# One visit a tile for the local attention jobs, and softmaxes four steps apart, in a fused attention and feed-forward kernel

## The chip, the cores and the metric

The kernel runs on one core of a Trainium2 chip. The core has a matrix engine (TensorE, called PE in the profile, with its weight loads as PEld), a vector engine (VectorE, DVE), a scalar engine (ScalarE, ACT), GpSimd (POOL) and SyncE (SP), whose queue issues the DMAs. The metric is the time of one execution on the device in microseconds (us); lower is better.

## The reference

Eight batches of eight heads, 576 positions, 64 channels, all float32. The first four heads of each batch attend to the last 32 positions (local); the other four attend to the earlier positions that are equal to the query's modulo 32 (strided). The attention output, 4608 tokens of 512 channels, goes through a feed-forward layer with an exact GELU of width 2048.

```python
def _attn_ref(q, k, v):
    stride = 32
    scores = (1.0 / np.sqrt(D)) * np.matmul(q, k.transpose(0, 1, 3, 2))
    rel = pos[:, None] - pos[None, :]
    mask_local = (rel >= 0) & (rel < stride)
    mask_strided = (rel >= 0) & (pos[None, :] % stride == pos[:, None] % stride)
    masks = [mask_local if h < H // 2 else mask_strided for h in range(H)]
    scores = np.where(masks, scores, -1e9)
    attn = softmax(scores)               # with 1e-9 added to the sum
    return np.matmul(attn, v)

def _moe_ref(x, w_in, w_out):            # x: 4608 x 512, from the attention
    h = x @ w_in
    g = 0.5 * h * (1.0 + erf(h / sqrt(2)))
    return g @ w_out
```

## The kernel before, in words

**Tiles and steps.** The 4608 tokens are 12 tiles of 384 (`TT`). The feed-forward layer has 16 blocks (`NF`) of 128 hidden units, so there are 192 steps; step `n` is block `n % 16` of tile `n // 16`, and `ready[t] = 16 t` is the first step of tile `t`. Numbers are split into a high and a low part, so each product takes three matmuls: `ffn_h(n)` (L602 to L604) makes 12 matmuls into one of two PSUM banks `H`; `ffn_g(n)` lets ACT apply the GELU in place (L611) and copy the high part `gh` (L613), and DVE subtract to the low part `gl` (L615); `ffn_o` (L641 to L643) makes 9 matmuls of step `n - 2` into the output banks `O0` to `O2`. Because `H` has two banks, `ffn_h(n + 2)` may begin only when `gl` of step `n` has been read out of its bank. At the end of a tile ACT copies the output out (L648) and SP stores it.

**Strided attention** is done on DVE, in units: dot products (L477), a softmax whose exponential is on ACT (L487), weighted sums (L517, L519), a transpose (L527) and the split into the tile's high and low part `xh`, `xl` (L231 on ACT, L233 on DVE). `run_strided` hands out this work step by step. Exponentials that are pending are issued by `flush_exps`; a GELU after an exponential needs another activation table (the ACT_TABLE_LOAD rows).

**Local attention** is done in jobs of 128 tokens, three to a tile (`JPT`), for tiles 2 to 11 by `band_job` (tiles 0 and 1 are done in the opening part by an order written out by hand). A job has seven parts, each ended by a `yield`: 0, the scores, 32 matmuls of 32 columns by 64 (L290) into the score banks `S0` and `S1`, of which job `i` uses columns `128 i` to `128 i + 127`; 1, the row extremes on DVE (L304); 2, the exponentials on ACT (L308); 3, sum, reciprocal, product and transpose on DVE (L311 to L314), and eight small DMAs (L319) that lay the probabilities out as a band; 4, the values, 16 matmuls (L328) into a bank `X`; 5, the copy of `xh` on ACT (L231); 6, the difference `xl` on DVE (L233). Of a tile, jobs 0 and 1 write their values to bank `X`, and job 2 takes a fresh tile in the bank of `S0`.

**What sets the order.** In the steady part, from step 16 on, the order of PE and of ACT is the order in which the program issues; the order of DVE, SP and POOL is left to a planner. `step(n)` first calls `visit(n)`, then `run_strided`, then `ffn_h(n)`, `ffn_g(n)` and `ffn_o(n - 2)`. `visit` does the local work of a step: for tile `t`, the scores and row extremes of all three jobs at step `ready[t-1] + 2`; the exponentials of job `i` `2 i + 1` steps later and part 3 `2 i + 2` steps later; the values and the split at `ready[t-1] + 12`. So PE leaves the feed-forward matmuls twice a tile, once for 96 matmuls and once for 48.

```python
SCORES, VALUES = 2, 12
score_at = {ready[t - 1] + SCORES: t for t in range(2, NTILE)}
value_at = {ready[t - 1] + VALUES: t for t in range(2, NTILE)}
```

Of the kernel before, what the change touches and what calls it, by code (L numbers as in the profile page):

```python
# [10 lines left out]
F32 = mybir.dt.float32  # L11
# [12 lines left out]
P = 128  # L24
STRIDE = 32
TT = 384
LU = 64
# [56 lines left out]
def attn_ffn_kernel(ctx: ExitStack, tc: tile.TileContext, qk, vl, qka, va, qs, ks, vs, w, out):  # L84
    nc = tc.nc
    NJ = qk.shape[0]
    NR, D = qs.shape[2:]
    S = NR * STRIDE
    HL = P // STRIDE
    NT, DM = out.shape  # L90
    NF = w.shape[0]
    NC = DM // P
    NU = len(PLACE)
    NV = len(VISITS)
    NTILE = NT // TT
    NS = NTILE * NF
    JPT = NJ // NTILE
    SC = 1.0 / (D ** 0.5)
    DH = D // 32
    N2 = HL // 2  # L100
# [20 lines left out]
    def rows(j):  # L121
        return slice(j * D, (j + 1) * D)
# [107 lines left out]
    def to_x(dh_, dl_, src):  # L230
        nc.scalar.copy(dh_, src)  # L231
        yield
        nc.vector.tensor_tensor(dl_, src, dh_.bitcast(F32), ALU.subtract)  # L233

    def local_job(x, banks=None, dve=0, pn=-1):
# [35 lines left out]
        dst = [a[:, 0:N2, c0:c0 + P] for a in x_tile(t)]  # L271
        yield from to_x(*dst, xv)

    def band_job(x, bt, sx):

        QB = STRIDE
        i = x % JPT
        if i == 0:  # L280
            sx["s"] = [ps_a.tile([P, DM], F32, name=f"S{j}_L{x}", tag=f"S{j}") for j in range(2)]
        s = [t[:, i * P:(i + 1) * P] for t in sx["s"]]
        qv = jq[x][:, 0:2 * N2 * LU].rearrange("p (r a t) -> p r a t", r=N2, a=2)
        kv = jq.pop(x)[:, 2 * N2 * LU:].rearrange("p (r a t) -> p r a t", r=N2, a=2)
        head = [(h % 2, slice(h // 2 * 2 * QB, (h // 2 + 1) * 2 * QB)) for h in range(HL)]
# [16 lines left out]
        for h in range(HL):  # L302
            j, cs = head[h]
# [14 lines left out]
                kb = g % 2 + c  # L318
                nc.sync.dma_start(bt[kb * QB:(kb + 1) * QB, g, :], tv[g * QB:(g + 1) * QB, c, :])  # L319
        yield  # L320
        if i % 2 == 0:
            sx["x"] = ps_a.tile([P, DM], F32, name=f"X_L{x}", tag="X" if i == 0 else "S0")
        xv = sx["x"][:, i % 2 * N2 * P:(i % 2 + 1) * N2 * P].rearrange("p (r q) -> p r q", r=N2)
        bv = bt.rearrange("p (a b) (h q) -> p a b h q", a=2, h=HL)
        for r in range(N2):
            for a in range(2):
                for j in range(2):
                    nc.tensor.matmul(xv[rows(j), r, a * LU:(a + 1) * LU], jv[x][:, a, 2 * r + j, :],  # L328
                                     bv[:LK, a, :, 2 * r + j, :], start=True, stop=True)
        jv.pop(x)  # L330
        load_jv(x + 3)
        yield
        t, c0 = divmod(x * P, TT)
        dst = [d[:, 0:N2, c0:c0 + P] for d in x_tile(t)]
        yield from to_x(*dst, xv)


    ka = {}
# [120 lines left out]
    def flush_exps(u):  # L459
        while exps and exps[0][0] <= u:  # L460
            exps.pop(0)[1]()
# [298 lines left out]

    SCORES, VALUES = 2, 12
    score_at = {ready[t - 1] + SCORES: t for t in range(2, NTILE)}
    value_at = {ready[t - 1] + VALUES: t for t in range(2, NTILE)}
    banks = {}
    local = {}
    band = slot("band", [P, 4 * DM])
# [4 lines left out]
    def part(x, *which):  # L773

        for p in which:
            if p == 0:
                local[x] = [band_job(x, bts[x % NBT], banks), 0]
            assert local[x][1] == p
            local[x][1] += 1
            if next(local[x][0], True) is not None:  # L780
# [111 lines left out]
```

## Time and profile before

| | us |
|---|---|
| runs | 888.6, 890.39, 4788.15 |
| median of the runs | 890.39 |
| the profiled execution: time | 890.2 |
| the profiled execution: span, first to last instruction | 888.4 |
| PE busy in the span | 860.2 (97%) |
| DVE busy | 714.1 (80%) |
| ACT busy | 461.2 (52%) |

The time of the profiled execution is 1.8 us more than its span; the trace shows nothing of that rest. The opening part with the hand-written order takes about the first 114 us; the 192 steps end at about 884 us. A "visit" below is one place at which PE does local matmuls between two steps.

### The profile page before, as it was taken

The page shows a single profiled execution, that of the slowest core. Times are in us where ns is not written, and L with a number is a line of the kernel's source. Part 1 is how long each engine was busy: PE and PEld are TensorE (multiplying, and loading weights), DVE is VectorE, ACT ScalarE, POOL GpSimd, SP SyncE. Part 2 cuts the span into 40 slices and gives each one's busy share as a digit, 9 for nine tenths or more (in the row PEclk, how much of TensorE's full clock was granted, in tenths as well). Part 3 has the DMA queues.
Part 4 walks back from the last instruction along what each step waited for, and adds up shares of the span by engine and source line. Part 5 has one row for each costly group of instructions (what it writes and reads, how often), then busy time and mean ns, then how long its engine had stood idle before and what let it go on. Part 6 is the DMA issues. An engine that isn't in the chain of part 4 may idle for free.

```text
span 888.4 us, 19181 instructions
## 1 busy us (share of the span) xinstructions
PE 860.2 (97%) x5948; PEld 771.0 (87%) x5948; DVE 714.1 (80%) x4894; ACT 461.2 (52%) x983; POOL 16.3 (2%) x86
## 2 busy tenths in 40 slices
PE   5499999999999999999999999999999999999998
PEld 4488889889889889988898988988888988999997
DVE  5999999689969989949989969969979988675111
ACT  5999765256446257246346436536534632733222
POOL 4000000000000000000000000000000000000000
PEclk9699999999999999999999999999999999999999
DMA  9992120221030213103022122012113011100101
GB/s 321 363 362 83 48 87 19 81 81 44 29 134 14 61 40 104 36 2 114 12 75 88 40 75 84 16 55 81 61 34 105 16 61 36 31 18 0 37 1 36
DMA packets 33399, 66.27 MB, mean 75 GB/s; under 512 B 6416, under 2 KB 15376, under 8 KB 31248
## 3 DMA queue, kind: packets, MB, share of 16 engines
q1 hardware_dynamic: 33296, 65.04, 22.6%
q8 instruction: 47, 0.77, 0.4%
q14 instruction: 56, 0.46, 0.2%
HBM read 51.64 MB, written 9.44 MB: 69 GB/s over the span
## 4 chain that ended last, share of the span: by engine, by line
PE 91%; DVE 4%; DMA 3%; ACT 1%; SPq 0%; issue 0%; DVEq 0%
PE H L602 15%; PE O L642 15%; PE H L604 15%; PE O L643 15%; PE H L603 15%; PE O L641 14%; DMA ws<-in_w_dram 2%; PE X_L L328 2%; DMA vl<-in_vl_dram 1%; PE S_L L290 1%; DVE acc L519 1%; DVE junk L477 1%; DVE ws L154 0%; DVE w L164 0%; DVE ws L156 0%
## 5 line engine op out<-in xcount | busy, mean ns | idle before, releaser
L611 ACT ACTIVATE H<-H 128x384 f32<-128x384 f32 x192 | 91.4, 476 | 352.8 <-PE H L604 315.6
L602 PE MATMUL H<-xh,w 128*128 128x384 f32 x768 | 262.5, 342 | 4.5 <-DVE gl L615 3.2
L604 PE MATMUL H<-xh,w 128*128 128x384 f32 x768 | 260.0, 338 | 0.0
L603 PE MATMUL H<-xl,w 128*128 128x384 f32 x768 | 259.2, 337 | 0.7 <-DVE xl L233 0.7
L519 DVE SCALAR_TENSOR_TENSOR acc<-sv,sc,acc 128x64 f32<-128x64 f32 x1158 | 258.3, 287 | 0.6
L643 PE MATMUL O<-w,gl 128*128 128x512 f32 x576 | 228.2, 396 | 0.0
L642 PE MATMUL O<-w,gh 128*128 128x512 f32 x576 | 227.7, 395 | 0.0
L641 PE MATMUL O<-w,gh 128*128 128x512 f32 x576 | 224.8, 390 | 0.0
L477 DVE CUSTOM_DVE_ANT_0 junk<-sq,sk 128x64 f32<-128x64 f32 x1290 | 214.5, 228 | 6.3 <-DMA sk<-in_ks_dram 6.2
L615 DVE TENSOR_TENSOR gl<-H,gh 128x384 fp32r<-128x384 f32 x192 | 107.4, 560 | 113.1 <-ACT gh L613 112.1
L602 PEld LDWEIGHTS H<-xh,w 128*128 128x128 f32 x768 | 144.9, 189 | 14.7 <-DVE gl L615 4.1
L603 PEld LDWEIGHTS H<-xl,w 128*128 128x128 f32 x768 | 145.0, 189 | 8.3 <-DVE xl L233 1.1
L604 PEld LDWEIGHTS H<-xh,w 128*128 128x128 f32 x768 | 144.9, 189 | 0.0
L643 PEld LDWEIGHTS O<-w,gl 128*128 128x128 f32 x576 | 108.1, 188 | 23.1
L642 PEld LDWEIGHTS O<-w,gh 128*128 128x128 f32 x576 | 108.3, 188 | 18.3
L641 PEld LDWEIGHTS O<-w,gh 128*128 128x128 f32 x576 | 108.5, 188 | 17.5
L477 DVE DVE_READ_ACCUMULATOR2_ANT sc<- 128x1 f32 x1290 | 118.8, 92 | 0.0
L613 ACT CAST gh<-H 128x384 fp32r<-128x384 f32 x192 | 92.2, 480 | 6.0
L611 ACT ACT_TABLE_LOAD x48 | 61.6, 1283 | 1.1 <-issue 0.3
L487 ACT ACT_TABLE_LOAD x35 | 44.9, 1283 | 0.6
L308 ACT ACTIVATE PT_L<-P_L,nm_L 128x64 f32<-128x64 f32 x120 | 40.0, 335 | 0.1
L517 DVE TENSOR_SCALAR acc<-sv,sc 128x64 f32<-128x64 f32 x132 | 25.9, 253 | 0.5 <-DMA sv<-in_vs_dram 0.2
(106 smaller groups left out, 509.6 us busy)
## 6 DMA issues: line engine op xcount, KB each, us to landing
ws<-in_w_dram SPq DMA_DIRECT2D x16, 1024.0 KB, 14.9
qk<-in_qk_dram SPq DMA_DIRECT2D x36, 320.0 KB, 4.7
out_dram<-ob SPq DMA_DIRECT2D x34, 256.0 KB, 2.6
vl<-in_vl_dram SPq DMA_DIRECT2D x36, 192.0 KB, 3.8
sk<-in_ks_dram SPq DMA_DIRECT2D x8, 576.0 KB, 5.0
sv<-in_vs_dram SPq DMA_DIRECT2D x8, 576.0 KB, 3.9
band<-PT_L SPq DMA_DIRECT2D x240, 16.0 KB, 1.8
sq<-in_qs_dram SPq DMA_DIRECT2D x4, 576.0 KB, 3.9
```

The lines of the kernel that those rows point to most:

```text
L477: nc.vector.tensor_tensor_reduce(junk, sq[vi, "q"][:, r0 + r, :], sq[vi, "k"][:, c, :], 1.0, 0.0, ALU.mult, ALU.add, ss[u][:, r, c:c + 1])
L487: exps.append((u, lambda: nc.scalar.activation(s, s, AF.Exp, scale=SC)))
L519: nc.vector.scalar_tensor_tensor(acc[:, r, :], sq[vi, "v"][:, c, :], wgt, acc[:, r, :], ALU.mult, ALU.add)
L602: nc.tensor.matmul(hp, w1[f][:, 0, c, :], xh[:, c, :], start=(c == 0), stop=False)
L603: nc.tensor.matmul(hp, w1[f][:, 0, c, :], xl[:, c, :], start=False, stop=False)
L604: nc.tensor.matmul(hp, w1[f][:, 1, c, :], xh[:, c, :], start=False, stop=(c == NC - 1))
L611: nc.scalar.activation(hp, hp, AF.Gelu)
L613: nc.scalar.copy(gh, hp)
L615: nc.vector.tensor_tensor(gl, hp, gh.bitcast(F32), ALU.subtract)
L641: nc.tensor.matmul(o, gh[:, sl], w2[f][:, 0, :], start=(f == 0), stop=False)
L642: nc.tensor.matmul(o, gh[:, sl], w2[f][:, 1, :], start=False, stop=False)
L643: nc.tensor.matmul(o, gl[:, sl], w2[f][:, 0, :], start=False, stop=(f == NF - 1))
```

## The change

For tiles 3 to 11 the scores are made in the visit that makes the values of the tile before them, at `ready[t-1] + 13` for the values of tile `t` and the scores of tile `t + 1`. Only tile 2's scores have a visit of their own (step 18, as before), and only tile 11's values. In a visit PE gets the value matmuls first, then the scores; the copies of the split come behind both. The row extremes leave the visit: of job `i` the parts 1, 2 and 3 are at 1, 2 and 3 steps after the scores, plus `4 i` (plus `2 i` for tile 2). The score banks are allocated by the visit, and the third job's values go to the unused last 128 columns of the next tile's two score banks, so that its split is two copies and two differences of 128 columns in place of one of 256. The loads of a job's queries and keys are asked for after part 0 and no longer after part 6. What is computed is the same.

```diff
     def band_job(x, bt, sx):
         QB = STRIDE
         i = x % JPT
-        if i == 0:
-            sx["s"] = [ps_a.tile([P, DM], F32, name=f"S{j}_L{x}", tag=f"S{j}") for j in range(2)]
-        s = [t[:, i * P:(i + 1) * P] for t in sx["s"]]
+        s = [t[:, i * P:(i + 1) * P] for t in sx[x // JPT]]
...
         yield
-        if i % 2 == 0:
-            sx["x"] = ps_a.tile([P, DM], F32, name=f"X_L{x}", tag="X" if i == 0 else "S0")
-        xv = sx["x"][:, i % 2 * N2 * P:(i % 2 + 1) * N2 * P].rearrange("p (r q) -> p r q", r=N2)
+        if i == 0:
+            sx["x"] = ps_a.tile([P, DM], F32, name=f"X_L{x}", tag="X")
+
+        xv = [sx["x"][:, (N2 * i + r) * P:(N2 * i + r + 1) * P] if i < 2 else sx[x // JPT + 1][r][:, JPT * P:]
+              for r in range(N2)]
...
-                    nc.tensor.matmul(xv[rows(j), r, a * LU:(a + 1) * LU], jv[x][:, a, 2 * r + j, :],
+                    nc.tensor.matmul(xv[r][rows(j), a * LU:(a + 1) * LU], jv[x][:, a, 2 * r + j, :],
...
-        dst = [d[:, 0:N2, c0:c0 + P] for d in x_tile(t)]
-        yield from to_x(*dst, xv)
+        if i < 2:
+            both = [(sx["x"][:, i * N2 * P:(i + 1) * N2 * P].rearrange("p (r q) -> p r q", r=N2), slice(0, N2))]
+        else:
+            both = [(xv[r], r) for r in range(N2)]
+        parts = [to_x(*[w_[:, d, c0:c0 + P] for w_ in x_tile(t)], src) for src, d in both]
+        for p in parts:
+            next(p)
+        yield
+        for p in parts:
+            next(p, None)
...
-    SCORES, VALUES = 2, 12
-    score_at = {ready[t - 1] + SCORES: t for t in range(2, NTILE)}
-    value_at = {ready[t - 1] + VALUES: t for t in range(2, NTILE)}
+    FIRST, VISIT = 2, 13
+    value_at = {ready[t - 1] + VISIT: t for t in range(2, NTILE)}
+    score_at = {ready[1] + FIRST: 2, **{n: t + 1 for n, t in value_at.items()}}
+    soft_at = {}
+    for n, t in score_at.items():
+        for i in range(JPT):
+            for p in (1, 2, 3):
+                soft_at.setdefault(n + p + i * (2 if t == 2 else 4), []).append((t * JPT + i, p))
...
     def visit(n):
-        for i in range(JPT):
-            for d, p in ((1, 2), (2, 3)):
-                t = score_at.get(n - 2 * i - d)
-                if t is not None:
-                    if p == 2:
-                        flush_exps(NU)
-                    part(t * JPT + i, p)
+        for x, p in soft_at.get(n, ()):
+            if x < NJ:
+                if p == 2:
+                    flush_exps(NU)
+                part(x, p)
+        t = value_at.get(n, 0)
         if n in score_at:
-            for p in (0, 1):
-                for i in range(JPT):
-                    part(score_at[n] * JPT + i, p)
-        if n in value_at:
-            for ps in ((4,), (5, 6)):
-                for i in range(JPT):
-                    part(value_at[n] * JPT + i, *ps)
+            banks[score_at[n]] = score_banks(score_at[n])
+        for i in range(JPT if t else 0):
+            part(t * JPT + i, 4)
+        for i in range(JPT if score_at.get(n, NTILE) < NTILE else 0):
+            part(score_at[n] * JPT + i, 0)
+        for i in range(JPT if t else 0):
+            part(t * JPT + i, 5, 6)
```

More of the change, by code (lines that the diff above doesn't have):

```diff
@@ L272, in local_job, with score_banks @@
         yield from to_x(*dst, xv)
+    def score_banks(t):
+        return [ps_a.tile([P, DM], F32, name=f"S{j}_{t}", tag=f"S{j}") for j in range(2)]
     def band_job(x, bt, sx):
@@ L779, in part @@
             local[x][1] += 1
-            if next(local[x][0], True) is not None:
+            next(local[x][0], None)
+            if p == 0:
                 load_jq(x + 3)
     def visit(n):
-        for i in range(JPT):
-            for d, p in ((1, 2), (2, 3)):
-                t = score_at.get(n - 2 * i - d)
-                if t is not None:
-                    if p == 2:
-                        flush_exps(NU)
-                    part(t * JPT + i, p)
-        if n in score_at:
-            for p in (0, 1):
-                for i in range(JPT):
-                    part(score_at[n] * JPT + i, p)
-        if n in value_at:
-            for ps in ((4,), (5, 6)):
-                for i in range(JPT):
-                    part(value_at[n] * JPT + i, *ps)
+        for x, p in soft_at.get(n, ()):
[4 more added lines that the diff above has]
+        t = value_at.get(n, 0)
+        if n in score_at:
+            banks[score_at[n]] = score_banks(score_at[n])
[5 more added lines that the diff above has]
+            part(t * JPT + i, 5, 6)
     def step(n):
```

## The prediction

> **What bounds the kernel now.** I began with the page: who is busy, and on what the chain that ended last lies.
>
> ```profile
> PE 860.2 (97%) x5948; PEld 771.0 (87%) x5948; DVE 714.1 (80%) x4894; ACT 461.2 (52%) x983; POOL 16.3 (2%) x86
> ...
> PEclk9699999999999999999999999999999999999999
> ...
> PE 91%; DVE 4%; DMA 3%; ACT 1%; SPq 0%; issue 0%; DVEq 0%
> ```
>
> PE is the bound, at a clock that is full nearly throughout; the 91% of the chain are PE's own instructions, one behind the other. The chain in order of time then tells what a tile costs, since each visit stands out as a long piece (start, length):
>
> ```profile
> 260.25 1.10 PE S_L L290 x71
> ...
> 303.42 1.59 PE X_L L328 x48
> ...
> 330.31 1.10 PE S_L L290 x71
> ```
>
> One tile takes 330.31 - 260.25 = 70.06 us, in which the two visits are the only pieces that aren't feed-forward matmuls. To price them I took PE's own timeline, first around a step without a visit, then around a score visit and a value visit of the neighbouring tiles:
>
> ```profile
> 405.68 0.33 PE L602 MATMUL H<-xh,w 128*128 128x384 f32 x1
> ...
> 407.78 0.39 PE L641 MATMUL O<-w,gh 128*128 128x512 f32 x1
> ...
> 409.63 0.39 PE L643 MATMUL O<-w,gl 128*128 128x512 f32 x1
> 409.86 0.33 PE L602 MATMUL H<-xh,w 128*128 128x384 f32 x1
> ```
>
> ```profile
> 399.95 0.40 PE L643 MATMUL O<-w,gl 128*128 128x512 f32 x1
> 400.28 1.17 PE L290 MATMUL S_L<-qk 64*32 64x64 f32 x96
> 401.38 0.45 PE L602 MATMUL H<-xh,w 128*128 128x384 f32 x1
> ...
> 403.60 0.39 PE L641 MATMUL O<-w,gh 128*128 128x512 f32 x1
> ```
>
> ```profile
> 373.08 0.40 PE L643 MATMUL O<-w,gl 128*128 128x512 f32 x1
> 373.41 1.62 PE L328 MATMUL X_L<-band,vl 96*64 96x64 f32 x48
> 374.96 0.44 PE L602 MATMUL H<-xh,w 128*128 128x384 f32 x1
> ...
> 377.17 0.39 PE L641 MATMUL O<-w,gh 128*128 128x512 f32 x1
> ```
>
> A plain step is 409.86 - 405.68 = 4.18 us, of which the twelve `H` matmuls take 2.10 and the nine `O` matmuls 2.08. The last `O` matmul is followed after 409.86 - 409.63 = 0.23 by the next `H`, but by a visit only after 0.33: an entry costs 0.10. The scores take 401.38 - 400.28 = 1.10 to the next `H`, whose twelve take 403.60 - 401.38 = 2.22, 0.12 too much. Score visit: 0.10 + 1.10 + 0.12 = 1.32. Value visit likewise: 0.10 + 1.55 + (2.21 - 2.10) = 1.76. Sixteen steps and both visits give 66.9 + 3.1 = 70.0, the tile's 70.06: nothing else is lost in a usual tile. So the change can win only at the visits, and in tiles that aren't usual.
>
> I looked for those by asking PE's timeline for `H` matmuls that waited, and ACT's for the reason. After the opening there is one:
>
> ```profile
> 636.50 0.40 PE L643 MATMUL O<-w,gl 128*128 128x512 f32 x1
> 637.82 0.44 PE L602 MATMUL H<-xh,w 128*128 128x384 f32 x1 [0.93 <-DVE gl L615]
> ```
>
> ```profile
> 634.73 0.41 ACT L231 CAST xh<-xs 128x256 fp32r<-128x256 f32 x1 [6.40 <-DVE xs L527]
> ```
>
> Here 637.82 - 636.50 = 1.32 stands in place of 0.23: 1.09 us lost. ACT stood 6.40 us behind a strided transpose that DVE had not reached, with GELUs queued behind it, and `H` had no free bank. This happens among the softmaxes of tile 9.
>
> **The visit.** Nine of the ten score visits (tiles 3 to 11) merge with a value visit; 48 + 96 matmuls stay. Removed is one return to feed-forward matmuls and one entry; added is one passage from values to scores, which the trace doesn't show. For its bounds I need where each group's last matmul starts:
>
> ```profile
> L290 PE MATMUL S_L<-qk x960: 212/216/240, 120.1 to 752.7; 64*32 64x64 f32 x192
> ...
> L328 PE MATMUL X_L<-band,vl x480: 222/222/270, 163.3 to 796.3; 96*64 96x64 f32 x160
> ```
>
> Last score: 400.28 + 1.17 - 0.216 = 401.23, so 0.95 after the first and 0.15 ahead of `H`. Last value: 373.41 + 1.62 - 0.222 = 374.81, 1.40 after the first and 0.15 ahead of `H`. With x for the passage, start to start, a merged visit is 0.10 + 1.40 + x + 0.95 + 0.15 + 0.12 = 2.72 + x, against 1.32 + 1.76 = 3.08: it saves 0.36 - x. Below, x can be the pitch within the values, 1.40/47 = 0.03; above, the largest change of shape shown, 0.33 into a visit. I take 0.15, since leaving a visit is also a change out of small matmuls and takes 0.15 from either group. That is 0.21 a tile, **1.9 us** for nine (ends 3.0 and 0.3; a loss would need a passage dearer than every one shown).
>
> The Trainium skill (TensorEngine Tiling, Key Properties) says that changing the tiling mode, not only the tile, drains TensorE; values and scores have different shapes, so it speaks against the merger being worth as much. A drain would be a whole last value matmul: x = 0.22, 0.14 a tile, 1.3 us for nine. No run here has shown that passage; the 0.15 out of a visit is less than a full matmul of 0.22, so the trace does not bear the rule out there.
>
> **The softmaxes.** The same thirty, with the same DVE instructions, elsewhere. What one job puts on DVE:
>
> ```profile
> L304 DVE CUSTOM_DVE_ANT_0 P_L<-S_L,bmaskNone 128x64 f32<-128x64 f32 x104 | 16.6, 222 | 3.2 <-PE S_L L290 1.7 <-ACT PT_L L308 1.4
> L314 DVE STREAM_TRANSPOSE PT_L<-PT_L 128x256 f32<-128x256 f32 x30 | 13.4, 447 | 0.0
> L313 DVE TENSOR_TENSOR PT_L<-PT_L,rs_L 128x256 f32<-128x256 f32 x30 | 12.7, 425 | 0.4 <-DVE rs_L L312 0.2 <-DVE m L485 0.2
> ```
>
> Four row extremes 4 x 16.6/104 = 0.64, product 0.42, transpose 0.45: 1.5 us, without the two short ones. Until now all three jobs lay at steps 2 to 8 of a tile; after, they lie at steps 14 to 16, then 2 to 4 and 6 to 8 of the next. DVE's load in the stretch with the stall, and in four of the stretches that get the first job:
>
> ```profile
> 611.50:646.30 34.80, 33.87 (x175) 30.39 (x170) 32.78 (x259) 22.71 (x51) 0.26 (x2) 1.00 0.26 83
> ```
>
> ```profile
> 243.30:255.90 12.60, 12.53 (x86) 1.00 0.26 95
> ...
> 383.40:396.00 12.60, 4.52 (x20) 1.00 0.01 1
> ...
> 664.80:677.40 12.60, 12.53 (x70) 1.00 0.09 20
> 734.90:747.40 12.50, 12.47 (x87) 1.00 0.01 2
> ```
>
> (In the first row the third busy time is DVE's, 32.78 of 34.80; in the others DVE alone.) Tile 9's job 0 goes out of that stretch, to steps 126 to 128, and takes 1.5 us with it; job 2's row extremes move from step 130 to 134, still ahead of the stall at step 136. The 1.5 is more than the 1.09 lost, so I count the stall as gone: **1.1 us**. What is late next there is the plain PE step. In exchange three stretches in which DVE is already full (243, 664, 734) get 1.5 us and one step with an exponential. What they can bear:
>
> ```profile
> 666.77 0.33 PE L604 MATMUL H<-xh,w 128*128 128x384 f32 x1
> ```
>
> ```profile
> 669.35 0.56 DVE L615 TENSOR_TENSOR gl<-H,gh 128x384 fp32r<-128x384 f32 x1
> ```
>
> `H` of that step ends at 667.10, `gl` at 669.91, 2.81 later; the bank is wanted one step and nine `O` matmuls on, 4.18 + 2.08 = 6.26. Adding 1.5 gives 4.3: covered. If DVE's backlog doubles that cover goes, and each further us is PE's.
>
> ACT: four exponentials and their table loads delay a GELU as before. Ten softmaxes load a table of their own now, twenty share one with a strided exponential:
>
> ```profile
> L308 ACT ACT_TABLE_LOAD x10 | 12.8, 1283 | 0.2
> ```
>
> If none shared, 20 x 2 x 1.283 = 51 us would come to ACT's 461 of 888, spread over twenty steps with room: nothing. The exponential of jobs 1 and 2 now comes one step behind its row extremes, where it had three and five; behind it on ACT wait the GELU and `gh`, and for these `gl` and `H`. Job 0 lived with one step already.
>
> **The split.** The third job's copy and difference become two of half the width, and the copies wait for scores to be issued ahead of them:
>
> ```profile
> L231 ACT CAST xh<-xs 128x128 fp32r<-128x128 f32 x8 | 2.4, 302 | 5.7 <-DVE xs L527 5.7
> L231 ACT CAST xh<-X_L 128x256 fp32r<-128x256 f32 x30 | 10.2, 375 | 29.1 <-PE X_L L328 21.6 <-DVE xl L233 7.5
> L233 DVE TENSOR_TENSOR xl<-X_L,xh 128x256 fp32r<-128x256 f32 x30 | 12.2, 426 | 6.6 <-ACT xh L231 6.6
> L233 DVE TENSOR_TENSOR xl<-xs,xh 128x128 fp32r<-128x128 f32 x8 | 2.3, 289 | 0.4 <-ACT xh L231 0.4
> ```
>
> ```profile
> 307.09 0.43 DVE L233 TENSOR_TENSOR xl<-X_L,xh 128x256 fp32r<-128x256 f32 x1
> ```
>
> ACT pays 2 x 302 - 375 = 229 ns more a tile, DVE 2 x 289 - 426 = 152. After the value visit of its tile at 303.4 the last `xl` was written at 307.5, 4.1 us later; with 1.1 us of scores ahead and 0.4 of extra work, 5.6. The next tile's first `H` comes three steps later, 12.5 us: hidden with 7 us to spare, nothing if that holds.
>
> **SP.** Each softmax issues eight band DMAs:
>
> ```profile
> band<-PT_L SPq DMA_DIRECT2D x240, 16.0 KB, 1.8
> ```
>
> They move with part 3, past the output stores early in a tile and the strided loads. The last job's now have five steps (21 us) to the values, and had four. Value and query loads serve the next visit, sixteen steps off. Nothing.
>
> **Sum.** Against the profiled execution's own 890.2 (its span 888.4 and 1.8 around it): 890.2 - 1.9 - 1.1 = **887.2 us**. The median 890.39 is practically that execution; the other undisturbed run, 888.6, shows a scatter of 1.8.
>
> **Rivals.**
> - *The passage drains.* As worked out: 890.2 - 1.3 - 1.1 = 887.8. For it: the shapes differ. Against: leaving a visit takes only 0.15. Chance 0.12.
> - *The planner keeps the stall.* DVE's order isn't written out; the spacing may not reach it, and ACT can stand behind the same strided transpose. 890.2 - 1.9 = 888.3. For it: the wait was on a strided transpose and not on a softmax. Chance 0.14.
> - *Slower: the first softmax lands where DVE is full.* Place: steps 14 to 16 of the tiles at 243, 664 and 734 us. If strided work there is already behind by more than 6.26 - 2.81 - 1.5 = 1.95 us when the visit comes (the 6.40 at tile 9 shows such backlogs), all that the job and the split add falls on PE: 1.5 + 2 x 0.426 + 2 x 0.289 = 2.9 us a tile, 8.7 for three, and 890.2 - 1.9 - 1.1 + 8.7 = 895.9; one such tile gives 890.1, no gain, and two make it slower (893.0). Against it: only one such wait in ten tiles so far. Chance 0.14, most of it for one or two tiles.
>
> **How the numbers follow.** My forecast has 0.58, the rivals 0.40, anything else 0.02. The low end is the forecast with x at 0.03 (886.1), less half the scatter: 885.2. The high end takes in the planner's case, and the slower rival with two tiles and a little scatter: 893.4. That leaves out about one in ten. Over 2%, about what a measurement of this kernel can tell from no change, is 17.8 us: all visits together are 10 x 3.08 = 30.8 us and their matmuls stay, so faster by that is all but excluded (0.01); slower by that needs over seven tiles at 2.9 (0.02).
>
> **What would show it.** PE's timeline has one visit a tile of about 2.87 us, entry and exit included, and the chain gives 69.85 us a tile; the `H` at about 635 us waits for nothing. The passage's x is read from the last L328 to the first L290. I am wrong if PE waits for `gl` or `xl` anywhere behind the opening, above all at steps 14 to 16, or if ACT's waits for row extremes grow until they reach `H`.

## The result, and the profile after

The changed kernel takes 897.91 us (median of 894.59 to 898.82) against 890.39 us before. Compared run by run the ratio is 1.0084, with a 95% interval of 1.0062 to 1.0105: slower by under one per cent, where the prediction had 887.2 us and a high end of 893.4. Under 2% it counts as no change, but the interval leaves no doubt of the sign. (One run of the kernel before, 4788.15 us, was disturbed and is left out of the ratio.) The profiled execution of the changed kernel took 897.91 us, with a span of 896.1.

Three lines of its page, the busy engines, the queue that brings instructions, and the chain that ended last:

```profile
PE 861.5 (96%) x5948; PEld 773.6 (86%) x5948; DVE 714.9 (80%) x4904; ACT 448.7 (50%) x983; POOL 16.7 (2%) x86
...
q8 instruction: 47, 0.77, 0.4%
...
PE 89%; ACT 3%; DVE 3%; DMA 3%; issue 1%; SPq 0%; ACTq 0%; DVEq 0%
```

PE has the same matmuls and is busy for about as long (861.5, was 860.2) in a span that is 7.7 us longer: the loss is idle time. "issue", time in which an engine waited for nothing that the profile shows, had 0% of the chain and now has 1%. Of PE's waits these are the ones that are new or grown (total, times, longest; the opening has one `gl` wait of its own in both kernels):

```profile
PE H L613 <- DVE gl L626: 6.5, 3, 3.8
...
PE H L614 <- issue: 2.0, 1, 2.0
...
PE H L613 <- issue: 1.2, 1, 1.2
```

The visit itself does what was forecast. PE's timeline at the first merged visit:

```profile
167.32 0.40 PE L654 MATMUL O<-w,gl 128*128 128x512 f32 x1
167.65 1.15 PE L331 MATMUL X_L<-band,vl 96*64 96x64 f32 x32
168.63 0.64 PE L331 MATMUL S<-band,vl 96*64 96x64 f32 x16
169.20 1.17 PE L291 MATMUL S<-qk 64*32 64x64 f32 x96
170.30 0.44 PE L613 MATMUL H<-xh,w 128*128 128x384 f32 x1
...
172.51 0.39 PE L652 MATMUL O<-w,gh 128*128 128x512 f32 x1
```

Values to scores 1.55, scores to `H` 1.10, the twelve `H` 2.21 in place of 2.10, and 0.10 for the entry: 0.10 + 1.55 + 1.10 + 0.11 = 2.86. The last value matmul starts at 168.63 + 0.64 - 0.222 = 169.05, so the passage x is 0.15. A tile without a wait, from one visit to the next in the chain in order of time (start, length), takes 307.39 - 237.55 = 69.84 us:

```profile
237.55 1.08 PE X_L L331 x32
...
307.39 1.08 PE X_L L331 x32
```

So the visits give back their 1.9 us, and something else costs over five times as much. I measured each step of PE's timeline behind the opening against a plain step (2.10 for `H`, 2.08 for `O`, the visits as above) and noted what was over by more than 0.15 us:

| place | before | after |
|---|---|---|
| step 25, `H` waits for `gl` | 0 | 0.94 |
| step 77, behind a merged visit, "issue" | 0 | 2.35, then 1.48 at half clock |
| step 135, `H` waits for `gl` | 1.09 | 3.95, then 1.63 at half clock |
| step 157, behind a merged visit, "issue" | 0 | 1.45 |
| sum | 1.09 | 11.80 |

That is +10.7, less 1.9 for the visits: +8.8. Measured from the first score matmul to the end, the two executions differ by 8.57; the opening was 0.85 shorter in this one execution. The account closes to about a quarter of a microsecond. (Below, "the steady time" is this time from the first score matmul to the end: 768.27 us before, 776.84 after. It leaves out the opening, which varies by about a microsecond from one execution to the next.)

**The two `gl` waits.** PE's timeline at the larger one, with two rows of ACT's timeline from the stretch before it, the copy at which ACT stood and the strided exponential from which that copy's data come (start, length, and in brackets the idle time before and what ended it):

```profile
638.93 0.40 PE L654 MATMUL O<-w,gl 128*128 128x512 f32 x1
643.12 0.44 PE L613 MATMUL H<-xh,w 128*128 128x384 f32 x1 [3.79 <-DVE gl L626]
```

```profile
616.45 0.24 ACT L498 ACTIVATE sc<-sc 128x48 f32<-128x48 f32 x1
...
640.03 0.41 ACT L231 CAST xh<-xs 128x256 fp32r<-128x256 f32 x1 [10.13 <-DVE xs L538]
```

643.12 - 638.93 = 4.19 stands in place of 0.23. It is the same wait as in the kernel before, on the same kind of instruction: ACT is at the strided split's copy, whose transpose DVE has not reached, and GELUs stand behind the copy. It stood 6.40 us before and stands 10.13 now.

What made it longer shows when the two traces are laid side by side. In the kernel before the same exponential is this row:

```profile
612.71 0.24 ACT L487 ACTIVATE sc<-sc 128x48 f32<-128x48 f32 x1
```

In both kernels it starts 6.59 us behind the first `H` matmul of step 129 (606.12 and 609.86): it did not move. Two other things did. The score visit that stood ahead of step 130 is now at step 125, so PE, without a wait, would come to `H` of step 136 22.72 us after the exponential, where it was 24.02. And the copy, 22.02 us after the exponential before (the row at 634.73 in the prediction), now comes after 23.58. DVE is busy in the stretch from the exponential to the transpose for nearly the same time, 21.25 of 21.53 us before and 21.39 of 23.10 now: the local work that left was replaced by strided work, and idle time came on top, most of it early in the stretch. There DVE's new order has the quotients of this softmax behind the sum of the next one, which waits for ACT, and the weighted sums begin 5.66 us after the exponential, where it was 3.70 (DVE's timeline, first before, then after; the 48 columns are this softmax, the 28 the next):

```profile
615.71 0.21 DVE L507 TENSOR_TENSOR sc<-sc,z 128x48 f32<-128x48 f32 x1
...
618.50 0.18 DVE L503 TENSOR_REDUCE z<-sc 128x2 f32<-128x28 f32 x1
```

```profile
620.56 0.18 DVE L514 TENSOR_REDUCE z<-sc 128x2 f32<-128x28 f32 x1 [0.84 <-ACT sc L498]
...
620.80 0.20 DVE L518 TENSOR_TENSOR sc<-sc,z 128x48 f32<-128x48 f32 x1
```

PE 1.30 us sooner and the copy 1.56 later make the 2.86 by which the wait grew. This is read from one execution of each kernel; no experiment takes the two parts apart.

The other wait is of the same kind, at the only tile whose softmaxes are two apart; here ACT stands 4.11 us and then has the exponentials of tile 2's third job and a table load to do before the next GELU:

```profile
148.79 0.41 ACT L231 CAST xh<-xs 128x256 fp32r<-128x256 f32 x1 [4.11 <-DVE xs L538]
```

```profile
154.89 0.44 PE L613 MATMUL H<-xh,w 128*128 128x384 f32 x1 [0.78 <-DVE gl L626]
```

**The two waits for "issue".** They fall a few matmuls behind the merged visits that start at 377.15 and 735.62, and at none of the seven others:

```profile
380.42 0.35 PE L613 MATMUL H<-xh,w 128*128 128x384 f32 x1
382.78 0.34 PE L614 MATMUL H<-xl,w 128*128 128x384 f32 x1 [2.01 <-issue]
...
740.78 0.34 PE L613 MATMUL H<-xh,w 128*128 128x384 f32 x1 [1.18 <-issue]
```

An engine that has its data and does not start may have run out of instructions. The trace has what is needed to look: every instruction of PE, and every transfer of the instruction queue. PE's queue holds 5948 matmuls, as many weight loads and 142 semaphore and drain instructions, 12,038; the page has 47 transfers (its q8) of 0.77 MB, 16 KB each; 12,038/47 = 256 instructions to a transfer. In stretches without a visit the transfers start 256 instructions apart, so the places at which a transfer is due can be counted (to within some ten instructions); "border" below is such a place. A plain step takes 42 instructions from its block in 4.19 us, a merged visit 296 in 2.86 us: more than a whole block, at ten times the rate. Before, a score visit took 192 and a value visit 104, ten steps apart. The place in its block at which each merged visit starts, and what PE lost behind it:

```
visit at step   29   45   61   77   93  109  125  141  157
place          145   93   41  245  193  141   89   37  241
lost, us         0    0    0  2.35   0    0    0    0  1.45
```

Only the two visits that begin a dozen instructions ahead of a border wait: they run through a whole block's worth inside the visit, and are out of instructions before the next transfer has come. In the first, the border is crossed at about 377.3; the transfer starts at 380.11, takes 1.17 us, and PE goes on at 382.78.

The waits themselves show that it is a block's end at which PE stands. Counted over PE's instructions in the trace, the stop comes behind number 5569 in the first and 10,433 in the second, both 193 above a multiple of 256, which is 294 (38 and a block) behind the border. The same holds for every such wait in the experiments below, 16 in all with these two: 5569 and 10,433, and in experiment 2, whose program is 104 instructions longer, 2753 and 7617, again 193 above a multiple of 256. In all 16, PE goes on 2.3 to 2.8 us after its transfer has started. What differs is the start of the transfer, 1.1 to 3.0 us behind the border, and so the wait. The next nearest case, place 193, crosses the border 63 instructions into the visit and leaves it with some 60 still ahead of the stop, which is 6 us at the rate of the plain steps: enough for any of these transfers. The loads that the visit itself asks for run in the same stretch; SP's timeline (start, length of the issue), and the windows around it (busy PE, PEld, DVE, ACT, POOL, then the granted clock, the share of the 16 DMA engines, GB/s):

```profile
377.88 1.28 SPq L190 DMA_DIRECT2D vl<-in_vl_dram  x3
379.27 2.38 SPq L184 DMA_DIRECT2D qk<-in_qk_dram  x3
```

```profile
380.60:384.00 3.40, 1.39 (x9) 1.24 (x9) 1.23 (x17) 0.00 (x0) 0.00 (x0) 1.00 0.91 300
384.00:387.40 3.40, 3.40 (x10) 2.73 (x10) 0.56 (x1) 0.95 (x2) 0.00 (x0) 0.51 0.10 36
387.40:390.80 3.40, 3.40 (x19) 3.17 (x18) 0.00 (x0) 0.67 (x2) 0.00 (x0) 0.99 0.00 0
...
643.50:646.90 3.40, 3.40 (x13) 3.40 (x12) 1.63 (x16) 2.81 (x7) 0.14 (x1) 0.50 0.00 0
```

The DMA engines are 91% busy while PE waits in this execution. And the clock column has the rest: in the window behind each long wait the granted clock is 0.51 and 0.50, and PE does 10 and 13 matmuls where the next window has 19. That is the 1.48 and the 1.63 of the table.

### The profile page after: what moved, and what is told of

Its sections match the earlier page's. It is cut to its first block, busy times and chain, and to the rows that moved or that the text cites. A ratio compares the mean times of both kernels' runs of the same rounds, so it can differ in the third digit from the quotient of the medians.

```text
span 896.1 us, 19214 instructions
## 1 busy us (share of the span) xinstructions
PE 861.5 (96%) x5948; PEld 773.6 (86%) x5948; DVE 714.9 (80%) x4904; ACT 448.7 (50%) x983; POOL 16.7 (2%) x86
## 4 chain that ended last, share of the span: by engine, by line
PE 89%; ACT 3%; DVE 3%; DMA 3%; issue 1%; SPq 0%; ACTq 0%; DVEq 0%
PE H L613 15%; PE H L615 14%; PE H L614 14%; PE O L653 14%; PE O L654 14%; PE O L652 14%; DMA ws<-in_w_dram 2%; DVE acc L530 1%; PE S L291 1%; PE X_L L331 1%; DMA vl<-in_vl_dram 1%; DVE junk L488 1%; ACT L622 1%; PE S L331 1%; ACT w L160 0%
## 5 line engine op out<-in xcount | busy, mean ns | idle before, releaser
L530 DVE SCALAR_TENSOR_TENSOR acc<-sv,sc,acc 128x64 f32<-128x64 f32 x1158 | 251.5, 277 | 0.6
L488 DVE CUSTOM_DVE_ANT_0 junk<-sq,sk 128x64 f32<-128x64 f32 x1290 | 208.2, 218 | 6.5 <-DMA sk<-in_ks_dram 6.5
L488 DVE DVE_READ_ACCUMULATOR2_ANT sc<- 128x1 f32 x1290 | 105.1, 81 | 0.0
```

The costliest lines, as they stand in the source:

```text
L488: nc.vector.tensor_tensor_reduce(junk, sq[vi, "q"][:, r0 + r, :], sq[vi, "k"][:, c, :], 1.0, 0.0, ALU.mult, ALU.add, ss[u][:, r, c:c + 1])
L530: nc.vector.scalar_tensor_tensor(acc[:, r, :], sq[vi, "v"][:, c, :], wgt, acc[:, r, :], ALU.mult, ALU.add)
```

## The experiments

Theory A, formed from this profile: the whole loss is made of the two kinds of waits; the "issue" waits come from 296 PE instructions in one burst, the `gl` waits from the new times of the softmaxes. The rivals: that the merged visit costs more than its matmuls show (banks, shapes); that the `gl` waits come from the burst too; and, later, that a wait comes from the copies' place on ACT rather than from DVE's work being late, and that the "issue" wait is a matter of DMA traffic alone. Ratios are against the kernel before on the same chip, whose medians lay between 889.2 and 890.0.

**1. Values and scores in visits of their own, one step apart.** The softmaxes stay where the change puts them.

```diff
     score_at = {ready[1] + FIRST: 2, **{n: t + 1 for n, t in value_at.items()}}
+    value_at = {n - 1: t for n, t in value_at.items()}
...
-        if n in score_at:
-            banks[score_at[n]] = score_banks(score_at[n])
+        if t or score_at.get(n) == 2:
+            banks[t + 1 if t else 2] = score_banks(t + 1 if t else 2)
```

> The changed kernel with its values at step 12 and its scores at step 13 of a tile, each in its own visit; softmaxes, banks and the split in two stay as changed. Theory A (PE runs out of instructions: it gets them in blocks of 256, and a merged visit takes 296 in 2.9 us): no PE wait put down to issue behind the opening, where the changed kernel has 2.0 us at 382 and 1.2 us at 738 us, and no half clock at 384. The visits cost 9 x 0.2 = 1.8 us more, the two lost stretches (2.35 + 1.48 + 1.45 = 5.3 us) are gone: about 3.5 us under the changed kernel, 894. The waits for gl at about 152 and 637 us stay, since the softmaxes stay. Rival (the issue waits come from something else in those two stretches): they stay, and the kernel is 1.8 us slower than the changed one, 899.5.

895.28 us, ratio 1.0066 [1.0042, 1.0090]; steady time 774.76. No "issue" wait is left behind the opening, and the `gl` waits stay:

```profile
640.87 0.45 PE L613 MATMUL H<-xh,w 128*128 128x384 f32 x1 [3.77 <-DVE gl L626]
```

```profile
PE H L613 <- DVE gl L626: 6.5, 3, 3.8
...
PE S L331 <- DMA band<-PT_L: 1.0, 1, 1.0
```

The second fence (PE's waits) has a new one: tile 2's values, now at step 28, came ahead of the last job's band, which cost 1.24. The account: 5.28 less for "issue", 1.9 more for the visits, 1.24 more here: 2.1; measured 776.84 - 774.76 = 2.08. So the bursts make the "issue" waits and only those, and merging the visits, good for 1.9, cost 5.3.

**2. A shift of the blocks.** Extra small matmuls (26, on a bank that is free) in the opening move every later visit within its block. A float32 matmul turned out to be two matmuls and two weight loads (the page has 6000 of each, were 5948), so the shift was 104 instructions, and not the 52 that the expectation counts on.

```diff
+        pad = ps_a.tile([P, DM], F32, name="pad", tag="X")
+        for _ in range(PAD):                       # PAD = 26
+            nc.tensor.matmul(pad[:, 0:32], ident, ident[:, 0:32], start=True, stop=True)
         for it in START:
```

> The changed kernel with 26 extra small matmuls (52 PE instructions with their weight loads) at the start of the opening, where PE waits for the first loads anyway; nothing else changes. In the trace of the changed kernel the merged visits at steps 29, 45, 61, 77, 93, 109, 125, 141, 157 begin, counted from the last boundary between blocks of 256 instructions, at places 145, 93, 41, 245, 193, 141, 89, 37, 241; only 245 and 241 waited. Theory A: all move by 52, to 197, 145, 93, 41, 245, 193, 141, 89, 37: PE waits for issue by about 2 us in the visit of step 93 (about 452 us) and nowhere else, steps 77 and 157 run through; about 2 to 3 us under the changed kernel. Rival (bound to those places of the schedule, or to the loads issued there): the waits stay at steps 77 and 157.

903.29 us, ratio 1.0143 [1.0105, 1.0181], but the opening became 6.3 us longer (first scores at 125.57, were 119.27), so the steady time is what compares: 772.74. PE's timeline at the only two "issue" waits behind the opening:

```profile
177.85 0.34 PE L615 MATMUL H<-xh,w 128*128 128x384 f32 x1 [0.59 <-issue]
...
527.78 0.33 PE L614 MATMUL H<-xl,w 128*128 128x384 f32 x1 [0.24 <-issue]
```

```
visit at step   29   45   61   77   93  109  125  141  157
place          249  197  145   93   41  245  193  141   89
lost, us      0.84   0    0    0    0  0.51   0    0    0
```

The step that the expectation names was missed, because the shift was twice as large; but the waits left steps 77 and 157 and went to the two visits that now start at 249 and 245, and to no other. The place in the block decides where. It does not decide how much: the same place 245 cost 2.35 above and 0.51 here.

**3. The strided split later.** The copy of a strided split is issued two steps after its transpose is emitted, or when the tile is due, so that ACT is not put behind a transpose that DVE has yet to reach.

```diff
-            splits.append((t, split, u))
+            splits.append((t, split, u, now[0]))
...
-        while splits and n >= xfree[splits[0][0]]:
+        now[0] = n
+        while splits and n >= xfree[splits[0][0]] and (n >= splits[0][3] + LATER or n >= ready[splits[0][0]]):
```

> The changed kernel with each strided split (copy of xh on ACT, difference on DVE) issued one step later than now, unless its tile begins. Theory B (ACT stands behind a strided transpose that DVE has not reached, with the GELUs behind it): the waits for gl at 152 us (0.94) and at 637 us (3.95, and 1.63 at half clock behind it) go, 6.5 us in all: about 891. The issue waits at steps 77 and 157 stay. Rival (DVE is simply behind there, and gl would be late whatever ACT waits for): at least 3 of the 4 us at 637 stay.

891.26 us, ratio 1.0011 [0.9990, 1.0032]; steady time 769.41, 7.4 less than the changed kernel: 5.2 of it at the `gl` waits, the rest because the "issue" wait at step 77 is shorter in this execution and no half clock follows it. PE's timeline at the one `gl` wait left in the steps:

```profile
644.08 0.45 PE L613 MATMUL H<-xh,w 128*128 128x384 f32 x1 [1.20 <-DVE gl L626]
```

The wait at step 25 is gone, the one at step 135 has shrunk from 3.95 to 1.36 (a step later), and no half clock follows. The "issue" waits stay, 1.08 and 1.42 us at steps 77 and 157. So ACT's place behind the transpose makes the waits, but not all of the second: the copy, now two steps after its transpose was emitted, still stands 4.54 us for it (at 637.98), with the exponentials of a local job and two table loads behind it.

**4. The softmaxes two steps apart in all tiles.**

```diff
-                soft_at.setdefault(n + p + i * (2 if t == 2 else 4), []).append((t * JPT + i, p))
+                soft_at.setdefault(n + p + i * 2, []).append((t * JPT + i, p))
```

> The changed kernel with the softmaxes two steps apart for all tiles (as for tile 2), the merged visits unchanged. The softmaxes of a tile then lie at steps 14 to 20 counted over, and tile 9's are done by step 132, ahead of the strided split at step 135. Theory C (spreading them four apart puts job 0 and job 1 into the chain of strided work from step 127 to 135 and makes the wait at 637 us longer): the wait there falls from 3.95 back to about 1 us or less, no half clock, about 4 us less. Rival (the planner's order of DVE moved for another reason, or the change of place to step 13): it stays above 3 us. The wait at 152 us stays in both, since tile 2 keeps its spacing; the issue waits at steps 77 and 157 stay.

888.47 us, ratio 0.9983 [0.9967, 0.9998]; steady time 766.92. The wait at step 135 is gone altogether, even the 1.09 of the kernel before, though ACT still stands 5.77 us at the same copy, which comes sooner (ACT's timeline of this kernel):

```profile
606.02 0.25 ACT L498 ACTIVATE sc<-sc 128x48 f32<-128x48 f32 x1
...
631.41 0.41 ACT L231 CAST xh<-xs 128x256 fp32r<-128x256 f32 x1 [5.77 <-DVE xs L538]
```

The strided exponential of 48 columns comes at 606.02 here and at 616.45 in the changed kernel. Part of that is only that this execution is 4.25 us ahead there; counted from the first `H` matmul of step 129 it is 0.41 in place of 6.59, 6.2 us sooner, and that is sooner than in the kernel before as well. DVE's busy time on weighted sums (L530) in steps 129 to 132, first of the changed kernel, then of this one (busy time and count, clock, DMA share, GB/s):

```profile
609.90:614.00 4.10, 0.86 (x4) 1.00 0.12 26
614.00:618.20 4.20, 0.00 (x0) 1.00 0.51 187
618.20:622.40 4.20, 0.00 (x0) 1.00 0.00 0
622.40:626.60 4.20, 1.82 (x8) 1.00 0.00 2
```

```profile
605.60:609.80 4.20, 0.88 (x4) 1.00 0.11 23
609.80:614.00 4.20, 1.79 (x8) 1.00 0.55 197
614.00:618.20 4.20, 2.28 (x11) 1.00 0.11 23
618.20:622.40 4.20, 2.27 (x10) 1.00 0.01 2
```

Together 2.68 us against 7.22. In the changed kernel DVE has next to no weighted sums to do for two steps, because their weights are not there, and then has them all to do when the transpose is due. This gives theory D: pending strided exponentials are issued by `flush_exps` ahead of a local job's exponentials. Two apart, a local job's exponentials fall on step 129 and take the strided one along, and with it the weighted sums, the transpose and the copy on which ACT stands. Four apart they fall on steps 127 and 131, and the strided one waits for its own turn in step 130, as in the kernel before. (The change in "issue" waits, 0.47 and 0.39 in place of 3.83 and 1.45, was not foreseen; the two visits still start ahead of a border.)

**5. The kernel before with the split later** (the edit of 3, on the kernel before).

> The kernel before (two visits a tile) with each strided split issued one step later, unless its tile begins. Theory B (ACT behind a strided transpose that DVE has not reached): the one wait for gl at 637 us, 1.09 us, goes, and nothing else changes: 0.9 to 1.1 us under the kernel before, a ratio of 0.999. Rival: the later split collides elsewhere, and as much is lost there.

889.34 us, ratio 0.9991 [0.9977, 1.0006]; steady time 767.40. The loss at step 135 goes from 1.09 to 0.32: the edit takes most of that wait in the kernel before as well, and is worth what it takes, under a microsecond.

**6. Two apart and the split later** (the edits of 4 and 3).

> The changed kernel with softmaxes two steps apart and each strided split one step later: the candidate for faster than both. If both causes are right, the waits for gl at 152 us (0.9) and at 637 us are gone together, and only issue waits in the visits of steps 77 and 157 stay (0.4 to 1.7 each, by what the loads beside them leave). From the first score visit to the end about 766 us, 2 us under the kernel before: a ratio of 0.997 to 0.998. Rival: the planner's new order of DVE makes a new wait, and it is no better than with two apart alone.

888.37 us, ratio 0.9984 [0.9971, 0.9996]; steady time 766.02. No `gl` wait is left in the steps; "issue" costs 0.74 at step 77 and 0.39 at step 157.

**7. Four apart, the pending exponentials early.** The local softmaxes stay as changed; `flush_exps` is also called where it would be if they were two apart. This is theory D against the rival that the local work itself, put later, holds up DVE.

```diff
+    flush_at = {n + 2 + 2 * i for n in score_at for i in range(JPT)}
...
         t = value_at.get(n, 0)
+        if n in flush_at:
+            flush_exps(NU)
```

> The changed kernel, softmaxes four apart, but with the pending strided exponentials issued 2, 4 and 6 steps behind the scores, where the version with two apart issues them along with its softmaxes. Theory D (four apart hurts by holding back the strided exponentials, whose weighted sums then start too late for the split at step 135): the wait at 637 us, 3.95 us and the half clock behind it, falls under 1 us. Rival (it is the local work of jobs 0 and 1 on DVE between steps 127 and 135): the wait stays above 3 us. The waits at 152 us and the issue waits at steps 77 and 157 stay.

One run: 887.22 us, span 885.4, steady time 768.31. The wait at step 135 is gone, with every local softmax where the change puts it. In ACT's timeline the exponential starts at 604.70, 0.41 us into step 129, and ACT stands 4.23 us at the copy:

```profile
604.70 0.25 ACT L498 ACTIVATE sc<-sc 128x48 f32<-128x48 f32 x1
...
628.56 0.41 ACT L231 CAST xh<-xs 128x256 fp32r<-128x256 f32 x1 [4.23 <-DVE xs L538]
```

Theory D holds: with the local softmaxes where the change puts them, issuing the strided exponentials sooner is enough to remove the wait. It does not say why the wait is longer than in the kernel before, whose exponential came no sooner than the changed kernel's. The waits at step 25 (0.92) and for "issue" (0.45 and 1.94) stay.

**8. Two apart for tile 9 alone** (`i * (2 if t in (2, 9) else 4)`).

> The changed kernel with two steps apart for the softmaxes of tile 9 alone (and of tile 2, as in the changed kernel). If the loss at 637 us is that one tile's own, it goes there, 4 to 5.6 us, and the waits at 152 us and in the visits of steps 77 and 157 stay. Rival (the planner's order of DVE has drifted over the tiles before it): the wait at 637 us stays above 3 us.

One run: 889.71 us, span 887.9, steady time 768.46. The wait at step 135 is gone, those at 25 (0.92), 77 (0.78) and 157 (1.74) stay. So the spacing of one tile of nine decides about the wait at step 135, and that of the others does not show.

**9. The two visits taken apart.** On top of 6, the values of tiles 5 and 10, whose visits are those of steps 77 and 157, are made a step earlier than the scores; the other seven visits stay merged.

```diff
+    value_at = {n - (t in (5, 10)): t for n, t in value_at.items()}
```

> The version with softmaxes two apart and later strided splits, and of the nine merged visits the two that PE enters shortly ahead of a block boundary (steps 77 and 157) taken apart again: their values one step earlier, in a visit of their own. Theory A: no issue wait is left; two separate visits cost 0.2 us each, and 0.4 to 1.9 us of issue waits in each go. From the first score visit to the end about 765.3 us against 766.0 with all nine merged and 768.3 for the kernel before: a ratio of about 0.997. Rival (the waits come from the steps, not from the burst): a wait stays at one of the two.

886.07 us, ratio 0.9963 [0.9949, 0.9977]; steady time 765.56. No step of PE behind the opening is more than 0.15 us too long; what PE's waits still list lies in the opening, the one wait for `gl` included:

```profile
PE H L613 <- DVE gl L626: 1.8, 1, 1.8
```

This one is faster than both kernels, by 0.37% (0.23 to 0.51) than the one before (under 2%, so it too counts as no change, with a clear sign). 767.18 (768.27 less its 1.09) less seven merged visits of 0.21 is 765.7; measured 765.56.

**10. Without the loads.** The changed kernel with the loads of the local jobs left out from tile 3 on: those jobs use tile 2's queries, keys and values again, so what it computes for them is not the reference's. It asks whether the "issue" wait comes with the DMA traffic (theory E) or is the burst's own (its rival).

```diff
-        if x < NJ and ("q", x) not in loaded:
+        if 9 <= x < NJ:
+            jq[x] = kept["q", x % 3]
+        elif x < NJ and ("q", x) not in loaded:
```

(and likewise for the values)

> The changed kernel with the loads of the local jobs' queries, keys and values left out from tile 3 on (the jobs of those tiles use tile 2's buffers, so their results are not the reference's); orders of PE and DVE as in the changed kernel. Theory E (the next block of instructions comes late because its transfer starts behind the loads that the visit itself sets off): the issue waits at steps 77 and 157, 2.0 and 1.2 us, fall to at most 0.4 each, and the half clock at 384 us goes, 4 to 5 us in all; the waits at 152 and 637 us stay. Rival (the burst alone is too fast for any fetch): both waits stay above 1 us.

892.08 us, ratio 1.0045 [1.0026, 1.0064]; steady time 773.06. PE's timeline (line numbers are six higher here):

```profile
379.28 0.33 PE L620 MATMUL H<-xl,w 128*128 128x384 f32 x1 [0.52 <-issue]
...
734.83 0.34 PE L619 MATMUL H<-xh,w 128*128 128x384 f32 x1 [0.60 <-issue]
```

Neither end: 2.01 became 0.52 and 1.18 became 0.60. The burst alone leaves about half a microsecond. That the rest came with the loads is not shown by this pair of traces. The kernel of experiment 8 has the loads, and its PE and SP do the same as the changed kernel's up to there; yet in its one execution the first wait is as short:

```profile
381.45 0.33 PE L614 MATMUL H<-xl,w 128*128 128x384 f32 x1 [0.52 <-issue]
```

So the first wait varies by 1.5 us between executions that have the same loads. What the loads do shows over all nine merged visits: without them, in this one trace, the transfer starts on average 1.3 us behind the border (1.05 to 1.73), and in the seven other traces with nine merged visits on average 1.7 to 2.2 (1.1 to 3.1). They put the transfers off, but by how much at one visit is open. The `gl` waits stayed (0.95, 3.95), so the loads have no part in them.

## Why the prediction was wrong

- **The visit** was right. x was taken at 0.15 and measured 0.15; a merged visit was to take 2.87 and takes 2.86, a tile 69.85 and took 69.84. The gain of 1.9 us is there, and experiment 9 cashes it. The Trainium skill (TensorEngine Tiling, Key Properties) says that a change of tiling mode drains TensorE; by the trace the passage costs 0.15, less than the 0.22 of a whole matmul, so that rival fell.
- **The stall at tile 9** is the step that failed: "Tile 9's job 0 goes out of that stretch, to steps 126 to 128, and takes 1.5 us with it ... so I count the stall as gone: 1.1 us". It grew from 1.09 to 3.95, and the idle time brought 1.63 more at half clock. Two terms were wrong. Job 0's 1.5 us left DVE's stretch, but the stretch did not get shorter by it: other strided work and 1.4 us more idle time filled it, since the weighted sums had to wait for their weights, and the copy came 1.56 us later after the strided exponential. And the score visit, which had kept PE busy ahead of step 130, left the same stretch, so PE wanted its bank 1.30 us sooner; that was counted as a gain of the visits and at nothing here. These two sizes are read from one trace of each kernel. What experiments show is what removes the wait: experiments 4, 7 and 8 each issue the strided exponential sooner, in step 129, and each take the whole wait away; experiment 3 shows that the copy's place on ACT is what passes most of DVE's delay on to PE.
- **ACT**: "The exponential of jobs 1 and 2 now comes one step behind its row extremes ... Job 0 lived with one step already" was counted at nothing. For tiles 3 to 11 that held. For tile 2 it cost 0.94: its third job's exponential now comes in step 24, right behind a strided split's copy at which ACT has stood 4.11 us; before, it came in step 23, and that copy, at 146.42, waited for nothing. Why DVE's transpose is later there was not followed. Experiment 3, which moves the split, takes that wait away; experiments 4, 7 and 8, which do not, keep it.
- **A term that is missing**: the supply of instructions. I priced the visit by the time of its matmuls and counted no instructions. Two of nine visits waited, 5.28 us in all with the half clock behind the first, nearly three times what merging gives (in the other traces with nine merged visits 0.9 to 3.0 us). Experiment 1 removes it by taking the visits apart, 2 moves it to other steps by shifting the blocks, 9 removes it by taking just those two visits apart.
- **SP**: "Value and query loads serve the next visit, sixteen steps off. Nothing." The data are in time, as said. But the loads run beside the transfers of instructions and put them off (experiment 10), by how much at one visit is open.
- **Steps 14 to 16 where DVE is full** (243, 664, 734 us): "4.3: covered" was right; none of them lost anything. The slower rival, at 895.9, came close to the measured time by another mechanism at another place. That strided work would be late was right as a kind; the place was the old one, so the closeness of the number is luck.
- **The planner's rival** kept the stall at its size. Its argument, that the wait was on a strided transpose and not on a softmax, was the right question: what sets the time of that transpose? I did not follow it back through the weighted sums to the exponential. DVE's order did change, and for the worse.
- **The split** was right: no tile's first `H` waits for `xl` behind the opening.
- **The range** ended at 893.4 since no case in it made the stall larger and none had a wait of PE on its instructions.

What stays open: why the "issue" wait at the same two visits was 0.47 and 0.39 in experiment 4 and up to 2.35 and 1.94 in other executions. It follows the start of the transfer (1.3 us behind the border at both in experiment 4, 2.8 and 3.0 at the longest), but what sets that start, beside the loads, was not separated. Nor was it settled how much of the account's last quarter of a microsecond is real.

## What to carry to other kernels

When work is moved, ask what its old place loses by it: here a visit that left gave PE 1.3 us less to do while a chain of other engines ran, and the DVE work that left did not shorten that chain, whose head is an exponential. Then list everything that a call issues: issuing pending exponentials one step sooner removed a wait that moving whole softmaxes did not. Follow the last wait on the path back until it reaches something that can be moved; its first cause may be four links away. Before many small matmuls are put into one burst, count the instructions: a burst longer than a block of instructions can starve the engine, and taking just the visits that do so apart keeps the gain of the others. Look at several executions before a wait's size is put down to one cause.

## What the runs showed of the hardware

- **Instruction supply.** 256 instructions (16 KB) came in one transfer, and PE ran dry, for 0.1 to 2.0 us, only where a merged visit of 296 instructions in 2.86 us began within a dozen or so of the place at which a transfer starts (places 241 to 249; 193 and below never). In 16 of 16 such waits it stopped at the same count within its blocks of 256, and went on 2.3 to 2.8 us after its transfer had started. The Trainium skill (Runtime: NRT & Kernel Launch, Instruction fetch mechanics) has blocks of 16 KiB or 256 instructions, which the trace bears out. The same section calls the cost of a border mostly hidden; that holds here for seven of nine visits and all plain steps, and does not hold for the two others.
- **Loads put the transfers of instructions off.** Over the nine merged visits the transfer started on average 1.3 us behind the border without loads and 1.7 to 2.2 with them. One wait alone does not show it: behind the same visit it was 0.52 us without loads, and with them 2.01 in one execution and 0.52 in another.
- **The clock.** After an idle time of 2.01 us the next 3.4 us window was granted 0.51, after 3.79 us 0.50; after 1.18 (step 157), 1.42 (experiment 3) and 1.69 us (experiment 7) PE lost nothing further. The Trainium skill (TensorE: Matmul & The Clock Gate, HAM oscillation) names gaps of more than about 3.4 us as what to avoid; here 2.01 us was enough, in the one case behind the opening that lies between 1.69 and 3.77.
- **A float32 matmul** counts as two matmuls and two weight loads in PE's queue: 26 more in the program were 104 more instructions.
